# A recurrence and a two-layer product on one core: v times its factors put into the outputs' bank by transposes, the factors copied by ScalarE, the third weights' load no longer held

## The chip, the cores and the metric

One core of a Trainium2 chip runs one program. The metric is the device time of one execution in microseconds (us); the time before is the median of three runs. The profile is of a further execution, taken by the hardware profiler. Engines: PE is TensorE, DVE is VectorE, ACT is ScalarE, POOL is GpSimd, SP is SyncE, which here issues the DMAs.

## What is computed

For 4 batches and 8 heads of width 48, over 768 steps of time:

```python
for t in range(S):
    cur = einsum('bhd,bhe->bhde', u[None] * kt, vt)
    y[:, :, t] = einsum('bhd,bhde->bhe', rt, state + cur)
    state = w[None, :, :, None] * state + einsum('bhd,bhe->bhde', kt, vt)
```

The y of all heads, as 3072 tokens of 384 features, goes through `h = x @ w_in` (2048 wide), a leaky ReLU with a slope per column, and `@ w_out`.

## The kernel before, in words

**Tiling.** Time is cut into `C = 6` chunks of 128 steps, heads into `P = 4` pairs, numbered q = 0 to 3. A chunk's four pairs give the x of its 4 x 128 tokens. The 2048 columns are 16 slices of 128, each with one weights' tile of 768 KB (its piece of `w_in` and of `w_out`). Step n is one slice for one chunk's tokens: `m_in(n)` is nine 128x512 products into a bank, ACT and DVE make the activation and split it in a high and a low part (`gh`, `gl`), and `m_out(n)`, three steps later, is nine products into the accumulators `acc0` to `acc2`, in three groups of three (gh with the high weights, gh with the low ones, gl with the high ones).

**Weights.** `weights(i)` turns raw tile i, 64-bit numbers, into a high part `wh` and a low part `wl`: on ACT `wx` (L356) and `wh` (L366), on DVE L358, L360, L363 and `wl` (L367). The raw tiles have two buffers (`wraw`), so load i waits until L363 has read tile i-2. The third tile (i = 2) is held by lines 340 to 343 as well: its load stands behind the small loads of `lower` that move 16 rows of the first chunk's x.

**The first chunk**, `first_chunk(q)`, runs before any product with weights. Per pair: DVE scales r and k (L459); DVE multiplies them (L531) and eight small products with u sum that over d (`c_sum`, L538) into eight columns of the tile `bank`, the factors of v; sixteen halves of products give the scores (L469); DVE writes `vc` = v times the factors (L475) and puts the scores over the mask (`copy_predicated`, L481); `out()` then puts scores times v (L491) and `vc` times the identity (L495) in one bank y. ACT and PE split y in a high and a low part (L406, L407, L409), and the state's products follow (L298, L302, L520). `with_warm` puts a product on the identity (L236) ahead of some pieces; it writes columns 128 to 511 of the same tile `bank`, to keep the array occupied.

**The later chunks** go pair by pair through `burst`, between steps: c_sum (only chunk 1), the factors to SBUF by ACT (`cu`, L543), eight copies by ACT of the identity times a factor (`base`, L590), the last pair's state times r (L644), its scores times v (L654), this pair's state (L616) and scores (L623). Half of L654, `through_scores(1)`, waits for an ACT piece that only touches y (`seen_y`, L669). Then come the new states T (L682, L687).

**The order** of each engine is a planner's (`Plan.in_order`): every piece has a cost in us and a rank, and among pieces that could start, the lowest rank goes first. The planner also adds L236 products where it sees PE idle. On the chip each engine runs its row in this order, and waits by semaphores.

Of the kernel before, what the change touches and what calls it, by code (L numbers as in the profile page):

```python
# [8 lines left out]
F32 = mybir.dt.float32  # L9
F32R = mybir.dt.float32r  # L10
I32 = mybir.dt.int32
U8 = mybir.dt.uint8
U32 = mybir.dt.uint32
AF = mybir.ActivationFunctionType
ALU = mybir.AluOpType
AX = mybir.AxisListType

B, H, S, D = 4, 8, 768, 48
L = 128
# [11 lines left out]

MM = 0.682
WARM = 0.16

# [145 lines left out]
def rwkv_prelu_kernel(ctx: ExitStack, tc, rk, vkr, wu, u, wall, alpha, w, r_all, k_all, v_all, oT):  # L180
    nc = tc.nc
# [10 lines left out]
    plan = Plan()  # L192
    add = plan.add

    def sb(shape, name, bufs, dt=F32, pool=None):
        return plan.buf(lambda: (pool or wk).tile(shape, dt, name=name, bufs=bufs), name, bufs)
# [52 lines left out]
    def load(out, fn, kb, rank, behind=()):  # L249
# [8 lines left out]
        rank=-100)  # L258
# [62 lines left out]

    raws, first_lower = {}, []

# [11 lines left out]
    def weights(i, need):  # L335


        if i not in raws:
            p = raw_weights(i, need - 9)
            if i == 2:  # L340

                for t, at in first_lower:
                    p.after.update(o for o, part, wr in plan.log[t] if wr and part == at and o.eng == "SP")
        raw = raws[i]
        h, l, t = wh[i], wl[i], sb([128, 2 * DM], "wx", 2, U32)

        def bits():
            return t()

        def x():  # L350
            return t().bitcast(F32)

        def hx():
            return h().rearrange("p k f -> p (k f)")

        add("ACT", 0.92, lambda: nc.scalar.activation(x(), raw()[:, :, 1].bitcast(F32), AF.Abs, scale=2.0 ** -112),  # L356
            r=[raw], w=[t], rank=need - 3 - 42 * (i == 0))
        add("DVE", 0.56, lambda: nc.vector.tensor_scalar(bits(), bits(), 3, None, op0=ALU.logical_shift_left), w=[t],  # L358
            rank=need - 2 - 42 * (i == 0))
        add("DVE", 0.95, lambda: nc.vector.scalar_tensor_tensor(  # L360
            out=bits(), in0=raw()[:, :, 0], scalar=29, in1=bits(), op0=ALU.logical_shift_right, op1=ALU.bitwise_or),
            r=[raw], w=[t], rank=need - 2 - 42 * (i == 0))
        add("DVE", 0.95, lambda: nc.vector.scalar_tensor_tensor(  # L363
            out=bits(), in0=raw()[:, :, 1], scalar=0x80000000, in1=bits(), op0=ALU.bitwise_and, op1=ALU.bitwise_or),
            r=[raw], w=[t], rank=need - 2 - 42 * (i == 0))
        add("ACT", 0.85, lambda: nc.scalar.activation(hx(), x(), AF.Copy), r=[t], w=[h], rank=need - 3 - 42 * (i == 0))  # L366
        add("DVE", 0.95, lambda: nc.vector.tensor_tensor(  # L367
            out=l().rearrange("p k f -> p (k f)"), in0=x(), in1=hx(), op=ALU.subtract), r=[t, h], w=[l], rank=need - 2 - 42 * (i == 0))
# [8 lines left out]
    def lower(c, k):  # L377
        for name, t in (("xh", xh[c]), ("xl", xl[c])):
            for g in range(2):
                to = slice(HI * g + D, HI * (g + 1))  # L380

                def dma(t=t, y=top[name], g=g, to=to):
                    nc.sync.dma_start(t()[to, k].bitcast(F32), y()[HI * g + 16 * k:HI * g + 16 * (k + 1)].bitcast(F32))

                first_lower.append((t, (k, g)))
                add("SP", 0.45, dma, r=[top[name]], w=[(t, (k, g))], rank=-40 if c == 0 else -8, kb=32)
# [58 lines left out]
    def first_chunk(q):  # L445
# [12 lines left out]
        for j, (t, tab) in enumerate(((r, lambda: W[q]()[:, None, 0:L]), (k0, lambda: W[q]()[:, None, L - 1::-1]))):  # L458
            add("DVE", 0.72, lambda t=t, tab=tab: nc.vector.tensor_tensor(  # L459
                out=t(), in0=t(), in1=tab().broadcast_to([112, B, L]), op=ALU.mult),  # L460
                r=[W[q]], w=[t], rank=10 * q + j - 90)
        first = diagonal(q, r, k0, None, bank, slice(8 * q, 8 * q + 8), (bank, q), 10 * q - 88, -95 + q, -70 + q)

        A = [psum() if q % 2 == 0 else pb([128, NT], f"acc{g}") for g in range(2)]

        def scores():
# [10 lines left out]
            in0=v().rearrange("p (g b) e -> p g b e", g=2), op=ALU.mult,  # L477
            in1=bank()[:, 8 * q:8 * q + 8].rearrange("p (b g) -> p g b", g=2)[:, :, :, None].broadcast_to([128, 2, B, D])),
            r=[v, (bank, q)], w=[vc], rank=10 * q - 77)
        for g in range(2):  # L480
# [6 lines left out]
        def out():  # L487
            for b in range(B):
                for g in range(2):
                    rows, x = (slice(0, HI) if g == 0 else half(g)), g * B + b  # L490
                    nc.tensor.matmul(y()[rows, b * L:(b + 1) * L], v().rearrange("p x e -> p (x e)")[  # L491
                        :, x * D:x * D + rows.stop - rows.start], base[g]()[:, b], start=b == 0,
                        stop=False, skip_group_check=True)
            for b in range(B):
                nc.tensor.matmul(y()[0:112, b * L:(b + 1) * L], vc().bitcast(F32)[:, b, 0:112], ident(), start=False,  # L495
                                 stop=b == B - 1, skip_group_check=True)

# [31 lines left out]
    def diagonal(q, r, k0, cu, sums, cols, mine, prod_rank, sum_rank, copy_rank):  # L529
# [11 lines left out]
        first = with_warm(1 if mine != sums else 0, 0.56, c_sum, r=[prod, uw], w=[mine], rank=sum_rank)  # L541
        if cu:
            add("ACT", 0.2, lambda: nc.scalar.activation(  # L543
                cu(), sums()[:, cols].rearrange("p (b g) -> p g b", g=2), AF.Copy), r=[mine], w=[cu], rank=copy_rank)
        return first
# [450 lines left out]
```

## Time and profile before

| what | value |
|---|---|
| median of 3 runs | 490.17 us (488.49 to 490.84) |
| the profiled execution | 492.12 us, span 490.4 us |
| PE busy | 478.5 us, 98% |
| DVE busy | 312.0 us, 64% |
| ACT busy | 239.2 us, 49% |
| mean granted clock of TensorE | 0.991 |
| HBM read and written | 36.38 MB and 6.29 MB |

The span runs from the first to the last instruction of the profiled execution; 1.7 us lie around it. Times in the rows are from the span's start. A granted clock of 1.00 is 2.4 GHz, 0.50 is 1.2 GHz. Products of fp32 are recorded twice each (x8 for four), transposes once.

### The profile page before, as it was taken

The numbers are of one execution on the slowest core, as the hardware profiler recorded it, in microseconds if no ns is written. First come the engines' busy times: TensorE is split into PE (matmuls) and PEld (weight loads), VectorE is DVE, ScalarE is ACT, GpSimd is POOL, SyncE is SP. The second block draws the span as 40 slices with busy tenths as digits, with TensorE's granted clock in tenths as the row PEclk, the third lists the DMA queues.
The fourth block names the chain that finished last, engine by engine and source line by source line (L and its number), as shares of the span: only waits on it lengthen the run. The fifth ranks groups of instructions, "written<-read, shape, count | busy, mean of one in ns | idle before, by whom it ended". The sixth has DMA issues, their size and how long they took to land.

```text
span 490.4 us, 11223 instructions
## 1 busy us (share of the span) xinstructions
PE 478.5 (98%) x4650; PEld 391.7 (80%) x4650; DVE 312.0 (64%) x522; ACT 239.2 (49%) x546; POOL 45.2 (9%) x51
## 2 busy tenths in 40 slices
PE   8998999999999999999999999999999999999994
PEld 4877887888888888888888888888888878888883
DVE  6897899999966787756646646646635534333331
ACT  5287677667464454534534634534633333433332
POOL 3000020003202011101102202102000000000000
PEclk9998899999999999999999999999999999999999
DMA  7656576463153353431212321312210000100002
GB/s 240 207 140 219 191 223 205 147 218 98 48 179 89 95 168 104 142 85 34 88 52 72 117 77 44 87 43 64 72 48 1 1 1 0 65 0 0 1 0 70
DMA packets 24616, 45.82 MB, mean 93 GB/s; under 512 B 3952, under 2 KB 11504, under 8 KB 24560
## 3 DMA queue, kind: packets, MB, share of 16 engines
q1 hardware_dynamic: 24416, 44.92, 29.9%
q8 instruction: 38, 0.62, 0.5%
q14 instruction: 18, 0.15, 0.1%
q10 hardware_dynamic: 144, 0.13, 0.1%
HBM read 36.38 MB, written 6.29 MB: 87 GB/s over the span
## 4 chain that ended last, share of the span: by engine, by line
PE 89%; DMA 4%; DVE 3%; ACT 2%; SPq 1%; issue 0%; ACTq 0%; DVEq 0%
PE acc L744 40%; PE bank L710 38%; DMA wraw<-wall 3%; PE bank L644 2%; PE bank L654 2%; PE bank L623 2%; PE bank L616 1%; DMA v<-vkr 1%; PE bank L495 1%; PE bank L491 1%; SPq L421 1%; DVE wx L363 1%; ACT wx L356 1%; PE acc L469 0%; DVE wl L367 0%
## 5 line engine op out<-in xcount | busy, mean ns | idle before, releaser
L719 DVE SCALAR_TENSOR_TENSOR g<-bank,alph,g 128x512 f32<-128x512 f32 x96 | 72.0, 750 | 108.5 <-ACT g L718 107.8
L718 ACT ACTIVATE g<-bank 128x512 f32<-128x512 f32 x96 | 57.3, 596 | 140.3 <-PE bank L710 140.1
L710 PE MATMUL bank<-xh,wh 128*128 128x512 f32 x288 | 113.1, 393 | 0.0
L710 PE MATMUL bank<-xh,wl 128*128 128x512 f32 x288 | 112.3, 390 | 0.5 <-DVE wl L367 0.5
L710 PE MATMUL bank<-xl,wh 128*128 128x512 f32 x288 | 112.1, 389 | 0.0
L723 DVE TENSOR_TENSOR gl<-g,gh 128x512 fp32r<-128x512 f32 x96 | 69.6, 725 | 42.0 <-ACT gh L722 41.1
L722 ACT ACTIVATE gh<-g 128x512 fp32r<-128x512 f32 x96 | 60.6, 631 | 65.7 <-DVE g L719 65.4
L744 PE MATMUL acc<-gh,wh 128*128 128x512 f32 x288 | 84.2, 399 | 0.0
L744 PE MATMUL acc<-gh,wl 128*128 128x512 f32 x288 | 83.4, 396 | 0.0
L744 PE MATMUL acc<-gl,wh 128*128 128x512 f32 x288 | 82.4, 392 | 0.0
L744 PEld LDWEIGHTS acc<-gh,wl 128*128 128x128 f32 x288 | 54.6, 191 | 11.7
L710 PEld LDWEIGHTS bank<-xh,wl 128*128 128x128 f32 x288 | 54.2, 188 | 11.9 <-DVE wl L367 0.8
L744 PEld LDWEIGHTS acc<-gl,wh 128*128 128x128 f32 x288 | 54.3, 189 | 11.5
L710 PEld LDWEIGHTS bank<-xh,wh 128*128 128x128 f32 x288 | 54.2, 188 | 11.5 <-ACT wh L366 0.2
L710 PEld LDWEIGHTS bank<-xl,wh 128*128 128x128 f32 x288 | 54.1, 188 | 11.5
L744 PEld LDWEIGHTS acc<-gh,wh 128*128 128x128 f32 x288 | 53.2, 189 | 11.4
L579 POOL TENSOR_TENSOR rr<-rr,kk 128x384 f32<-128x384 f32 x16 | 22.6, 1410 | 290.0 <-DMA kk<-vkr 213.4
L590 ACT ACTIVATE base<-ident,cu 128x64 f32<-128x64 f32 x160 | 41.4, 337 | 3.4 <-DVE cu L585 3.3
L396 DVE TENSOR_TENSOR xl<-bank,xh 48x256 fp32r<-48x256 f32 (+1 forms) x66 | 28.4, 430 | 1.6 <-ACT xh L395 0.2
L565 DVE TENSOR_TENSOR raw<-raw,W 112x512 f32<-112x512 f32 x40 | 26.6, 682 | 1.3 <-DMA raw<-rk 1.3
L395 ACT ACTIVATE xh<-bank 48x256 fp32r<-48x256 f32 (+1 forms) x66 | 25.4, 385 | 2.2 <-PE bank L654 1.0
L654 PE MATMUL bank<-base,v 64*48 64x64 f32 x640 | 19.1, 216 | 1.8 <-ACT seen_y L669 1.8
(106 smaller groups left out, 381.4 us busy)
## 6 DMA issues: line engine op xcount, KB each, us to landing
raw<-rk SPq DMA_DIRECT2D x46, 224.0 KB, 3.5
wraw<-wall SPq DMA_DIRECT2D x10, 768.0 KB, 6.3
v<-vkr SPq DMA_DIRECT2D x24, 192.0 KB, 3.5
wraw<-wall SPq DMA_DIRECT2D x12, 384.0 KB, 3.6
rr<-vkr SPq DMA_DIRECT2D x16, 192.0 KB, 2.5
kk<-vkr SPq DMA_DIRECT2D x16, 192.0 KB, 3.4
oT<-o SPq DMA_DIRECT2D x12, 256.0 KB, 2.3
oT<-g SPq DMA_DIRECT2D x5, 256.0 KB, 2.4
```

The costliest lines, as they stand in the source:

```text
L395: add("ACT", us, lambda: nc.scalar.activation(to(h), view(), AF.Copy), r=[src], w=refs(h), rank=rank)
L396: add("DVE", us + 0.1, lambda: nc.vector.tensor_tensor(out=to(l), in0=view(), in1=to(h), op=ALU.subtract), r=[src] + refs(h), w=refs(l), r ...
L565: add("DVE", 0.72, lambda t=t, tab=tab: nc.vector.tensor_tensor(out=t().rearrange("p b (j t) -> p (b j) t", t=span), in0=t().rearrange("p ...
L579: add("POOL", 1.2, lambda: nc.gpsimd.tensor_tensor(out=rt(), in0=rt(), in1=k(), op=ALU.mult), r=[k] + ([wh[12]] if c == 2 else []), w=[rt] ...
L590: add("ACT", 0.32, lambda g=g, b=b: nc.scalar.activation(base()[:, g, b], ident2(), AF.Copy, scale=cu()[:, g, b:b + 1]), r=[cu, ident2], w ...
L654: nc.tensor.matmul(where(g, b, j), v0()[s, g * B + b], base0()[s, g, b], start=False, stop=(crossed == 1 and e == 0), skip_group_check=True)
L710: nc.tensor.matmul(hp()[:, :], a[i]()[:, k], x[c]()[:, k], start=(k == 0 and j == 0), stop=(k == NK - 1 and j == 2))
L718: add("ACT", 0.6, lambda: nc.scalar.activation(g(), hp()[:, :], AF.Copy), r=[hp], w=[g], rank=n - 100)
L719: add("DVE", 0.75, lambda: nc.vector.scalar_tensor_tensor(out=g(), in0=hp()[:, :], scalar=alph()[:, i:i + 1], in1=g(), op0=ALU.mult, op1=A ...
L722: add("ACT", 0.64, lambda: nc.scalar.activation(gh(), g(), AF.Copy), r=[g], w=[gh], rank=n - 100)
L723: add("DVE", 0.73, lambda: nc.vector.tensor_tensor(out=gl(), in0=g(), in1=gh(), op=ALU.subtract), r=[g, gh], w=[gl], rank=n - 99)
L744: nc.tensor.matmul(banks[k](), a[i]()[:, NK + k], x(), start=(begin and j == 0), stop=(end and j == 2))
```

## The change

Three things. `out()` writes `vc` into y first, by four transposes, and then adds scores times v; before, four fp32 products with the identity came last. The factors of the first chunk are copied by ACT into a tile `cu`, and DVE makes `vc` from that copy, not from `bank`. The third weights' load no longer stands behind the loads of `lower`; for tiles 2 and 3 the planner is told that they land 4 us later than its DMA model says (`late`), which changes its order alone. The diff, cut to its core (a branch for a list `BY_ACT`, which is empty, is left out, and in `weights` the reads of `raw` carry part numbers, for the planner alone):

```diff
         if i not in raws:
             p = raw_weights(i, need - 9)
-            if i == 2:
-
-                for t, at in first_lower:
-                    p.after.update(o for o, part, wr in plan.log[t] if wr and part == at and o.eng == "SP")
+            if i in (2, 3):
+                p.late = 4.0
...
-                first_lower.append((t, (k, g)))
...
-        first = diagonal(q, r, k0, None, bank, slice(8 * q, 8 * q + 8), (bank, q), 10 * q - 88, -95 + q, -70 + q)
+        cu = sb([128, 2, B], "cu", 2)
+        first = diagonal(q, r, k0, cu, bank, slice(8 * q, 8 * q + 8), (bank, q), 10 * q - 88, -95 + q, -70 + q)
...
-            in1=bank()[:, 8 * q:8 * q + 8].rearrange("p (b g) -> p g b", g=2)[:, :, :, None].broadcast_to([128, 2, B, D])),
-            r=[v, (bank, q)], w=[vc], rank=10 * q - 77)
+            in1=cu()[:, :, :, None].broadcast_to([128, 2, B, D])), r=[v, cu], w=[vc], rank=10 * q - 77)
...
         def out():
             for b in range(B):
+                nc.tensor.matmul(y()[0:112, b * L:(b + 1) * L], vc().bitcast(F32)[:, b, 0:112], ident(), start=b == 0,
+                                 stop=False, is_transpose=True, skip_group_check=True)
+            for b in range(B):
                 for g in range(2):
                     rows, x = (slice(0, HI) if g == 0 else half(g)), g * B + b
                     nc.tensor.matmul(y()[rows, b * L:(b + 1) * L], v().rearrange("p x e -> p (x e)")[
-                        :, x * D:x * D + rows.stop - rows.start], base[g]()[:, b], start=b == 0,
-                        stop=False, skip_group_check=True)
-            for b in range(B):
-                nc.tensor.matmul(y()[0:112, b * L:(b + 1) * L], vc().bitcast(F32)[:, b, 0:112], ident(), start=False,
-                                 stop=b == B - 1, skip_group_check=True)
+                        :, x * D:x * D + rows.stop - rows.start], base[g]()[:, b], start=False,
+                        stop=b == B - 1, skip_group_check=True)
...
-        if cu:
-            add("ACT", 0.2, lambda: nc.scalar.activation(
-                cu(), sums()[:, cols].rearrange("p (b g) -> p g b", g=2), AF.Copy), r=[mine], w=[cu], rank=copy_rank)
+        add("ACT", 0.2, lambda: nc.scalar.activation(
+            cu(), sums()[:, cols].rearrange("p (b g) -> p g b", g=2), AF.Copy), r=[mine], w=[cu], rank=copy_rank)
```

The change moves instructions on every engine but POOL. Line numbers after the change are 1 to 10 higher. Three places matter.

PE at pair 1 of the first chunk, with what each instruction waits for: c_sum, the product on the identity, and the scores. Before:

```order
L236 MATMUL acc_140<-ident 128x384
L538 MATMUL acc_140<-uw,g 64x2 [waits DVE_49]
L538 MATMUL acc_140<-uw,g 64x2 x7
L236 LDWEIGHTS ident
L236 MATMUL acc_140<-ident 128x384 [waits DVE_49]
L469 MATMUL acc_267<-raw 128x128 [waits DMAHW4_49,DMAHW3_49]
```

After (L237 is L236, L548 is L538, L480 is L469):

```order
L237 MATMUL acc_140<-ident 128x384
L548 MATMUL acc_140<-uw,g 64x2 [waits DVE_49]
L548 MATMUL acc_140<-uw,g 64x2 x7
L237 LDWEIGHTS ident
L237 MATMUL acc_140<-ident 128x384
L480 MATMUL acc_269<-raw 128x128 [waits DMAHW4_49,DMAHW3_49]
```

The second product on the identity waited for DVE before, and waits for nothing now (`acc_140` is the tile `bank`).

SP from the last small loads of the first chunk's x on; `v` and `raw` are the later chunks' inputs. Before:

```order
L383 DMA xl<-xl 16x512 x2
L423 DMA v<-vkr 128x384 x4
L577 DMA rr<-vkr 128x384
L327 DMA wraw<-wall 128x1536 x2
L421 DMA raw<-rk 112x512 x2
L327 DMA wraw<-wall 128x1536
```

After:

```order
L394 DMA xl<-xl 16x512 x2
L328 DMA wraw<-wall 128x1536
L433 DMA v<-vkr 128x384 x4
L586 DMA rr<-vkr 128x384
L328 DMA wraw<-wall 128x1536 x2
L431 DMA raw<-rk 112x512 x2
```

The third weights' load moved ahead of five loads; the fifth's moved ahead of two.

ACT around the second burst, from the activation copy of step 1 (`g`) on. Before:

```order
L718 ACTIVATE g<-bank 128x512
L356 ACTIVATE wx<-wraw 128x768
L302 ACTIVATE kk<-bank 128x192 x2
L722 ACTIVATE gh<-g 128x512
L669 ACTIVATE seen_y<-bank 1x2
L356 ACTIVATE wx<-wraw 128x768
```

After:

```order
L727 ACTIVATE g<-bank 128x512
L362 ACTIVATE wx<-wraw 128x768
L303 ACTIVATE kk<-bank 128x192 x2
L731 ACTIVATE gh<-g 128x512
L552 ACTIVATE cu<-bank 128x8
L696 ACTIVATE T<-T,one 112x192
L599 ACTIVATE base<-ident,cu 128x64 x5
L678 ACTIVATE seen_y<-bank 1x2
```

`seen_y` and now T stand behind the third tile's `wx` and what follows it. On PE the second step's products come partly ahead of the first burst, with two more products on the identity before them, and two groups of `m_out(0)`, not one, ahead of the second burst.

## Rows read from the trace of the kernel before

**Rows 1.** Waits of PE from 9 to 100 us: total, times, longest.

```profile
PE bank L654 <- ACT seen_y L669: 1.8, 1, 1.8
PE acc L236 <- DVE gh L475: 0.7, 1, 0.7
PE bank L710 <- DVE wl L367: 0.5, 1, 0.5
```

**Rows 2.** Stretches: busy us (instructions) of PE, PEld, DVE, ACT, POOL; clock; DMA share, GB/s.

```profile
10.00:28.00 18.00, 17.29 (x228) 14.28 (x227) 14.45 (x25) 6.63 (x15) 0.00 (x0) 1.00 0.70 216
28.00:42.00 14.00, 12.79 (x292) 10.84 (x291) 11.63 (x22) 9.55 (x28) 0.00 (x0) 1.00 0.67 206
...
44.00:51.00 7.00, 6.98 (x45) 5.69 (x46) 7.00 (x13) 5.89 (x15) 0.00 (x0) 0.55 0.52 167
51.00:60.00 9.00, 9.00 (x157) 7.53 (x156) 7.04 (x11) 4.71 (x8) 0.00 (x0) 0.97 0.48 153
60.00:100.00 40.00, 39.50 (x368) 31.63 (x367) 38.80 (x60) 28.78 (x61) 3.02 (x2) 1.00 0.67 206
100.00:400.00 300.00, 300.00 (x3094) 248.24 (x3093) 193.96 (x333) 146.85 (x352) 38.02 (x30) 1.00 0.27 80
```

**Rows 3.** The chain that ended last, 34 to 45 us: start, length, what.

```profile
34.54 7.37 DMA wraw<-wall
...
41.93 0.89 ACT wx L356
...
43.80 0.17 ACT seen_y L669
```

**Rows 4.** PE in order of time, 10 to 35 us: start, length, instructions [idle before].

```profile
10.85 0.63 PE L538 MATMUL acc<-uw,g 112*64 112x2 f32 x16
12.19 0.32 PE L236 MATMUL acc<-ident 128*128 128x384 bf16 x1 [0.71 <-DVE gh L475]
...
13.54 0.60 PE L298 MATMUL bank<-ident,raw 112*128 112x112 f32 x4
14.07 1.09 PE L491 MATMUL bank<-base,v 128*64 128x128 f32 x16
...
19.25 1.13 PE L495 MATMUL bank<-ident,gh 128*112 128x128 f32 x8
20.21 0.33 PE L236 MATMUL acc<-ident 128*128 128x384 bf16 x1
...
27.69 0.55 PE L298 MATMUL bank<-ident,o 112*128 112x112 f32 x4
28.00 0.46 PE L407 MATMUL bank<-xh,minus 112*112 112x512 f32 x1
...
34.74 0.63 PE L616 MATMUL bank<-v,kk 64*64 64x48 f32 x31 [0.82 <-ACT kk L302]
```

**Rows 5.** Groups by line and shape, 9 to 100 us: busy, mean ns | idle before.

```profile
L475 DVE TENSOR_TENSOR gh<-v,acc 128x384 f32<-128x384 f32 x4 | 2.2, 551 | 3.4 <-PE acc L236 2.1 <-PE acc L538 1.3
...
L687 ACT ACTIVATE T<-T,one 112x192 f32<-112x192 f32 x4 | 1.8, 446 | 0.0
...
L543 ACT ACTIVATE cu<-bank 128x8 f32<-128x8 f32 x4 | 0.7, 174 | 0.8 <-PE bank L538 0.8
```

**Rows 6.** The chain that ended last, 0 to 12 us.

```profile
5.03 6.46 DMA v<-vkr
```

**Rows 7.** The chain that ended last, around 102 us.

```profile
102.17 1.36 PE bank L710 x6
```

**Rows 8.** SP's queue in order of time, 29 to 36 us.

```profile
29.65 1.23 SPq L383 DMA_DIRECT2D xl<-xl  x2
30.98 3.00 SPq L423 DMA_DIRECT2D v<-vkr  x4
...
34.54 0.86 SPq L327 DMA_DIRECT2D wraw<-wall  x2
```

**Rows 9.** Line 327, the loads of whole weights' tiles.

```profile
DMA to landing us min/median/max: 4.3/7.4/9.9
```

More of the change, by code (lines that the diff above doesn't have):

```diff
@@ L32 @@
 MM = 0.682
+BY_ACT = ()
 WARM = 0.16
@@ L320, in half_table @@
             pt()[:, :].rearrange("p (m g e) -> p m g e", m=P, g=2)[:, :, :, 0:D], AF.Copy), r=[pt], w=[whalf], rank=-62)
-    raws, first_lower = {}, []
+    raws = {}
     def raw_weights(i, rank, behind=()):
@@ L354, in hx @@
             return h().rearrange("p k f -> p (k f)")
-        add("ACT", 0.92, lambda: nc.scalar.activation(x(), raw()[:, :, 1].bitcast(F32), AF.Abs, scale=2.0 ** -112),
[L357 to L362, printed above, removed]
+        early = 42 * (i == 0)
+        by_act = i in BY_ACT
+        if by_act:
+            add("ACT", 0.9, lambda: nc.scalar.activation(
+                raw()[:, :, 0].bitcast(I32), raw().rearrange("p f a -> p (f a)").bitcast(U8).rearrange("p (f a) -> p f a", a=8)[:, :, 3],
+                AF.Copy, scale=1.0 / 32, bias=-31.0 / 64), w=[(raw, 0)], rank=need - 3 - early)
+        add("ACT", 0.92, lambda: nc.scalar.activation(x(), raw()[:, :, 1].bitcast(F32), AF.Abs, scale=2.0 ** -112),
+            r=[(raw, 1)], w=[t], rank=need - 3 - early)
+        if by_act:
+            add("DVE", 0.95, lambda: nc.vector.scalar_tensor_tensor(
+                out=bits(), in0=bits(), scalar=3, in1=raw()[:, :, 0], op0=ALU.logical_shift_left, op1=ALU.bitwise_or),
+                r=[(raw, 0)], w=[t], rank=need - 2 - early)
+        else:
+            add("DVE", 0.56, lambda: nc.vector.tensor_scalar(bits(), bits(), 3, None, op0=ALU.logical_shift_left), w=[t],
+                rank=need - 2 - early)
+            add("DVE", 0.95, lambda: nc.vector.scalar_tensor_tensor(
+                out=bits(), in0=raw()[:, :, 0], scalar=29, in1=bits(), op0=ALU.logical_shift_right, op1=ALU.bitwise_or),
+                r=[(raw, 0)], w=[t], rank=need - 2 - early)
         add("DVE", 0.95, lambda: nc.vector.scalar_tensor_tensor(
             out=bits(), in0=raw()[:, :, 1], scalar=0x80000000, in1=bits(), op0=ALU.bitwise_and, op1=ALU.bitwise_or),
-            r=[raw], w=[t], rank=need - 2 - 42 * (i == 0))
+            r=[(raw, 1)], w=[t], rank=need - 2 - early)
         add("ACT", 0.85, lambda: nc.scalar.activation(hx(), x(), AF.Copy), r=[t], w=[h], rank=need - 3 - 42 * (i == 0))
```

## The prediction, on record before the changed kernel ran

> **What bounds the kernel now.** I read the waits of PE first, then a table of stretches, then the chain of waits, then the timelines of PE and SP where the change puts its hand.
>
> From 100 to 400 us PE is busy in every microsecond and the clock stands at 1.00 [rows 2]. There time is PE's own work, the change touches none of it, and whatever PE is early or late at 100 us reaches the end unchanged. So the question is what happens before 100 us.
>
> There PE has few waits: 1.8 us in a burst, until ACT has run `seen_y`; 0.7 us of a product on the identity, until DVE has made `vc`; 0.5 us for a `wl` [rows 1]; and 0.82 us ahead of the first burst [rows 4]. The first is the dear one. From 44 to 51 us, just behind it, the mean granted clock is 0.55, between the level of 2.4 GHz and that of 1.2 GHz; before and after it is 1.00 or close to it [rows 2]. Seven microseconds at 0.55 lose 7 x 0.45 = 3.2 us. The chain of waits says where it comes from: the third weights' load is issued at 34.54 and lands 7.37 us later, only then ACT can run `wx` (41.93), and `seen_y`, for which PE waits, stands in ACT's row behind that (43.80) [rows 3]. Stall and slow stretch cost 5.0 us together.
>
> DVE is the second bound. From 60 to 100 us it is busy for 38.80 of 40 us [rows 2], making weights that PE needs in turn. PE can get ahead there only as far as DVE does.
>
> **The transposes.** Four times, eight recorded products of `vc` with the identity go, and four transposes come. The eight took 0.96 us from their start to the next instruction's (19.25 to 20.21). Four transposes of 112 columns took between 0.31 us (27.69 to 28.00) and 0.53 us (13.54 to 14.07) [rows 4]; for 128 columns that is 0.35 to 0.61. Saved: 0.35 to 0.61 each, 1.4 to 2.4 in all. I take the middle of the two, 0.5 each, **2.0 us**. PE ran through this stretch without waiting, so it is PE's time. They stand first in `out()` now and wait for `vc`; but DVE writes `vc` ahead of the masked copies that L491 waited for already, so that wait is no new one.
>
> **The false wait.** L236 writes columns of `bank` that nobody else reads, yet it waited 0.71 us for DVE's `vc`, which reads other columns of that tile [rows 4], and `vc` waited for the first v, issued at 5.03 and landed 6.46 us later [rows 6]. Now ACT reads the tile, right behind c_sum; the printed order shows that product without a wait. **0.7 us.** The four copies cost ACT 174 ns each by the same copy elsewhere [rows 5]; ACT was busy for 6.63 of 18 us here [rows 2]. Without that cover each would delay the next `vc` by 0.2 us.
>
> **What DVE gets.** It sat idle 3.4 us ahead of its four `vc`. Of that 2.1 us was behind PE and goes; 1.3 us is the first v's landing, though the row names PE, and stays [rows 5].
>
> **The first burst.** PE comes 2.7 us earlier. The 0.82 us for `kk` [rows 4] were short work ahead of a busy ACT; two products on the identity, 0.33 us each [rows 4], and part of the next step stand there now. **0.2 us** gained, between 0 and 0.8.
>
> **The third weights' load.** SP issued the four v at 30.98, behind the last small load, and the weights at 34.54 [rows 8]. In the new order the weights come where the v stood, and SP's row up to there follows PE and ACT, which are some 2.5 us early: so at about 28.6. With the median landing of such loads, 7.4 us, it is there at 36.0, with the best, 4.3 us, at 32.9 [rows 9]. Before it was 41.91, so it is at least 5.9 us earlier, while PE would be earlier by 2.7 and the stall's 1.8, which is 4.5. So the load is no longer the last to come. **The 1.8 us stall goes**, and with it what the clock lost, **3.2 us**.
>
> What is late next: the printed order puts `T` behind `gh` and the factors in ACT's row, and PE's second burst begins with products that read T. From the end of c_sum that is a copy of factors, 0.17 us, and T, 0.45 us [rows 5], with the latencies some 0.75 us in which PE has nothing else (an estimate). I charge **0.75 us**, between 0 and the 1.8 of the old stall. The old waits of 0.7 and 0.82 us did not bring the clock down, so I keep it at 1.00.
>
> **DVE's cap.** Ahead of 60 us DVE is idle for 3.6 us from 10 to 28, 2.4 from 28 to 42 and 2.0 from 51 to 60 [rows 2]; less the 1.3 for the first v that is 6.7 us, and it can lose hardly more. PE already waits 0.5 us for a `wl` [rows 1]. If PE wants to be 7 us early and DVE manages 6.7, that wait grows: **0.3 us**.
>
> **Sum**: 2.0 + 0.7 + 0.2 + 1.8 - 0.75 + 3.2 - 0.3 = 6.85, say 6.9 us. The profiled execution took 492.12 us, so its like would take 485.2. It is 2.0 us above the median of 490.17; I take the same gain from the median: **483.3 us**. With all terms at their good ends (2.4, 0.7, 0.8, 1.8, 3.2, no charge) the gain is 8.9, so 481.3; with the poor ones (1.4, 0.7, 0, a new wait as long as the old stall, 3.2, and 1.0 for DVE) it is 4.3, so 485.9.
>
> The flag's path is moved too (its count on PE, three small DVE instructions, SP's load of it), to some 230 us, where PE has no wait. I cost it at nothing; SP's loads there are for bursts several steps ahead.
>
> **A rule that speaks against it.** In the trace transposes of k stand at 13.54 and at 27.69 [rows 4], in a stretch whose clock is 1.00 [rows 2]: these few did not bring it down, and I count no loss. The Trainium skill, "TensorE: Matmul & The Clock Gate", Part 4 (PE-mode transpose), says that a transpose does not count as busy for the clock as a product does. By that, 16 transposes in place of 32 recorded products thin the stretch from 12 to 28 us, and the sum would lose the 3.2 us of one slow stretch; by the rows it loses nothing.
>
> **Rivals.**
>
> *The clock falls all the same*, after the new wait for T, or among the transposes. For it: it fell once after 1.8 us without work. Against: shorter gaps left it alone. The price is the 3.2 us of rows 2, the gain 6.9 - 3.2 = 3.7: 486.5 us. Where the transposes alone are the cause (the page's rule above), the price and the time are the same. 18 in 100, of which 5 are for the rule.
>
> *The transposes cost what the products did.* An fp32 product is recorded twice; if these transposes are as well, 2.0 falls away: gain 4.9, 485.3 us. Against: all transposes in the trace are recorded once [rows 4]. 6 in 100.
>
> *The first v comes late: no gain, or slower.* The third weights' 768 KB now lie ahead of the v that the first burst needs. PE was at that burst at 34.74 - 0.82 = 33.9; it comes 2.7 earlier, but with two products on the identity (0.66), a c_sum (0.63 [rows 4]) and six products of the next step (1.36 [rows 7]) put ahead, so at 33.9 again. If the weights take 7.4 us (36.0 [rows 9]) and this v's 128x384 numbers 0.9 us more at 216 GB/s [rows 2], PE stands for 3.0 us, and the clock falls there instead. Then 2.7 early, 0.82 for the old wait and 1.8 for the old stall stand against 0.66, 3.0 and 0.75, and the 3.2 stays lost: a gain of 0.9, 489.3 us. Each microsecond more costs one: from a v that lands after 37.8 on, the kernel is slower than before; with the longest landing, 9.9 us, v is there at 39.4 and the time is 491.8 us. For it: the median landing. Against: that median stems from loads issued next to others, while this one has SP's queue nearly to itself; 4.3 us and a v at 33.8 are nearer. 9 in 100, of which 4 end slower by over 0.5%.
>
> **How the numbers follow.** The main case has 67 in 100 and lies from 481.3 to 485.9. The range for 8 in 10 takes it whole, with the dear transposes and the clock's case, whose own ends are as far apart: 480.5 to 488.5; the 0.8 below is for the profiled execution's distance from the median, half of which may be time that the median never lost or lost elsewhere. 0.5%, 2.45 us, is about what a measurement of this kernel can tell from no change. Faster by more (below 487.7) are the main case, the dear transposes and 11 of the clock's 18: 0.84. The same are 7 of the clock's and 5 of the late v's: 0.12. Slower: 0.04.
>
> **What would show it.** Right: the four transposes at the head of each `out()` recorded once; L236 without a wait for DVE near 12 us; the third weights landed before ACT's `wx` wants them; no PE wait near 42 us over 1 us, a short one on T; clock 1.00 from 10 to 100 us; PE in 100 to 400 full, all 7 us earlier. Wrong: a clock under 1.00 in any of these stretches; PE waiting for v or `kk` at the first burst; waits for `wl` above 1 us from 50 to 80 us, which would say that DVE caps it lower.

## The result and the profile after

| | before | changed |
|---|---|---|
| median | 491.17 us (488.49 to 492.61, 6 runs) | **484.77 us** (484.29 to 485.34, 6 runs) |
| the profiled execution | 492.12 us, span 490.4 | 485.22 us, span 483.4 |
| mean granted clock | 0.991 | 0.996 |

The ratio is 0.9873, interval [0.9843, 0.9903]: faster by 1.0 to 1.6%. The forecast of 483.3 us was 1.5 us too low, and the measured median lies inside its range. The profiled execution gained 6.90 us, where the sum had 6.85; the runs below show that several of its terms had other sizes or did not come, so that the sum came out this near is in part luck.

The waits of PE from 9 to 100 us in the changed kernel (total, times, longest), where [rows 1] stood:

```profile
PE bank L299 <- ACT T L535: 0.4, 1, 0.4
PE bank L663 <- ACT seen_y L678: 0.2, 1, 0.2
PE bank L504 <- DVE base L491: 0.2, 1, 0.2
PE bank L499 <- DVE gh L486: 0.2, 1, 0.2
```

The 1.8 us for `seen_y` and the 0.7 for `vc` at the product on the identity are gone. The stretches of [rows 2], same columns:

```profile
10.00:28.00 18.00, 17.68 (x264) 13.97 (x264) 16.57 (x27) 9.39 (x23) 0.00 (x0) 1.00 0.81 228
28.00:42.00 14.00, 13.56 (x266) 10.85 (x265) 13.20 (x26) 11.97 (x37) 0.00 (x0) 1.00 0.56 193
...
44.00:51.00 7.00, 7.00 (x146) 5.85 (x145) 6.93 (x11) 3.78 (x8) 0.00 (x0) 1.00 0.91 283
51.00:60.00 9.00, 9.00 (x84) 7.13 (x84) 8.35 (x14) 7.71 (x19) 0.79 (x1) 1.00 0.83 230
60.00:100.00 40.00, 39.68 (x334) 32.46 (x329) 38.79 (x56) 26.47 (x51) 1.96 (x2) 1.00 0.61 194
100.00:400.00 300.00, 300.00 (x3149) 247.35 (x3148) 193.02 (x333) 145.64 (x354) 36.58 (x30) 1.00 0.25 77
```

The clock stands at 1.00 in every one; what is left under 1.00 is the tail (0.50 from 480 us on), after PE's last product, while the last results are stored. DVE is now busy for 16.57 of the 18 us from 10 to 28 (14.45 before): more of its work falls into this stretch.

PE in order of time, pair 1 of the first chunk and both bursts (start, length, instructions, [idle before]), where [rows 4] stood:

```profile
14.84 0.34 PE L237 MATMUL acc<-ident 128*128 128x384 bf16 x1
...
17.03 0.65 PE L499 MATMUL bank<-ident,gh 128*112 128x128 f32 x4
17.60 1.09 PE L504 MATMUL bank<-gl,v 128*64 128x128 f32 x16
...
34.30 0.62 PE L625 MATMUL bank<-v,kk 64*64 64x48 f32 x30
...
38.07 0.63 PE L548 MATMUL bank<-uw,g 112*64 112x2 f32 x16
38.63 1.14 PE L653 MATMUL bank<-raw,T 48*48 48x64 f32 x32
```

The four transposes take 0.57 us from their start to the next instruction's. The first burst (34.30) starts without a wait, and so does the second: the products that read T (38.63) follow c_sum directly. DVE's T of the first burst, then ACT around the second burst, same columns:

```profile
35.90 0.40 DVE L691 SCALAR_TENSOR_TENSOR T<-T,one,bank 112x192 f32<-112x192 f32 x1
```

```profile
36.88 0.89 ACT L362 ACTIVATE wx<-wraw 128x768 f32<-128x768 f32 x1
...
38.83 0.45 ACT L696 ACTIVATE T<-T,one 112x192 f32<-112x192 f32 x1
...
40.49 0.17 ACT L678 ACTIVATE seen_y<-bank 1x2 f32<-1x2 f32 x1
```

The third weights (issued at 28.98, SP's row) are there before ACT wants them at 36.88: no wait ahead of `wx`, where ACT before had to wait for them until 41.93 [rows 3].

### The profile page after: what moved, and what is told of

The parts are those of the page before. It is cut to its first block, busy times and chain, and to the rows that moved or that the text cites. A ratio compares the mean times of both kernels' runs of the same rounds, so it can differ in the third digit from the quotient of the medians.

```text
span 483.4 us, 11208 instructions
## 1 busy us (share of the span) xinstructions
PE 474.7 (98%) x4636; PEld 387.6 (80%) x4636; DVE 313.0 (65%) x522; ACT 238.5 (49%) x550; POOL 42.9 (9%) x51
## 4 chain that ended last, share of the span: by engine, by line
PE 93%; DMA 2%; DVE 2%; ACT 1%; SPq 1%; issue 0%; ACTq 0%; DVEq 0%
PE acc L753 41%; PE bank L719 40%; PE bank L653 3%; PE bank L663 2%; PE bank L632 2%; PE bank L625 2%; DMA v<-vkr 1%; SPq L431 1%; PE bank L504 1%; PE bank L548 0%; DMA xl<-xl 0%; PE bank L299 0%; ACT xl L419 0%; ACT wh L377 0%; ACT kk L303 0%
## 5 line engine op out<-in xcount | busy, mean ns | idle before, releaser
L753 PE MATMUL acc<-gh,wl 128*128 128x512 f32 x288 | 82.0, 391 | 0.0
L588 POOL TENSOR_TENSOR rr<-rr,kk 128x384 f32<-128x384 f32 x16 | 20.2, 1265 | 285.3 <-DMA kk<-vkr 196.3
L574 DVE TENSOR_TENSOR raw<-raw,W 112x512 f32<-112x512 f32 x40 | 27.7, 711 | 2.8 <-DMA raw<-rk 2.8
L684 DVE COPY_PREDICATED base<-strict,bank 128x256 f32<-128x256 uint8 x40 | 17.2, 441 | 4.7 <-PE bank L632 4.4
```

The source lines that it names most:

```text
L588: add("POOL", 1.2, lambda: nc.gpsimd.tensor_tensor(out=rt(), in0=rt(), in1=k(), op=ALU.mult), r=[k] + ([wh[12]] if c == 2 else []), w=[rt] ...
L684: add("DVE", 0.42, lambda g=g: nc.vector.copy_predicated(base()[:, g], strict2()[:, None, :].broadcast_to([128, B, HI]), A[g]()[:, 0:256]. ...
L753: nc.tensor.matmul(banks[k](), a[i]()[:, NK + k], x(), start=(begin and j == 0), stop=(end and j == 2))
```

## The experiments

The kernel before is run again beside each group, and its own median moves: 490.22 (32 runs), 490.55 (23 runs), 489.51 (11 runs). It is read against the mean granted clock of each execution. Where that is 0.996 or more, before took 488.0 to 488.6 us; at 0.993 or 0.994 mostly 488.6 to 490.1; at 0.989 to 0.991 mostly 490.2 to 492.9. The changed kernel has 0.995 or 0.996 in all six, and they lie within 1.1 us. Whether an execution without a profile had a slow stretch, a stretch of several us at 0.50 before PE's last product, is inferred from this mean: of the fourteen profiles of this document, the nine with a mean of 0.996 or more have none, and the five with 0.990 to 0.995 have one each. So there are two things to explain: some 3.3 us between executions with no slow stretch, and what slow stretches add to the median. Since before's median moves, kernels are compared below by their own times. By the ratios a difference can come out a microsecond larger: the transposes are 2.2 us by them and not 0.95, with intervals that overlap.

**The transposes.** The changed kernel with products in their place; every engine's order stays.

```diff
-                                 stop=False, is_transpose=True, skip_group_check=True)
+                                 stop=False, skip_group_check=True)
```

> The changed kernel with the four products of vc with the identity in the transposes' place, first in out(); the order of every engine is the changed kernel's, row for row. Theory (a transpose is cheaper than two passes of an fp32 product): out() is 0.4 to 0.5 us longer for each of the four pairs, so PE comes 1.6 to 2.0 us later to the first step and the time is 486.4 to 486.8 against 484.8. Rival 1 (DVE caps PE between 50 and 80 us, PE's time in the prelude is slack): the four are longer in the trace but the time moves by less than 0.7. Rival 2 (transposes cost what products cost): no difference in the trace either. The clock stays at 1.00 from 10 to 100 us by all of them.

Measured: 485.72 us (485.09 to 487.52, 9 runs), ratio to before 0.9917 [0.9891, 0.9943]. PE at pair 1, in order of time:

```profile
16.96 1.13 PE L499 MATMUL bank<-ident,gh 128*112 128x128 f32 x8
18.01 1.09 PE L504 MATMUL bank<-gl,v 128*64 128x128 f32 x16
```

1.05 us against 0.57: nearly half a microsecond at a pair, as the prediction had it, 1.9 in four. But the median is lower than expected, 0.95 us above the changed kernel's, and the first `m_in` starts at 30.21 and not 28.84 (1.4 us). Pair 0 gives nothing: PE waits there 0.15 and 0.17 us for DVE's `gh` and `base` in the changed kernel, behind the first v's landing, and not at all in this one, whose pair 0 is done at 14.77 (the changed kernel's at 14.84, shown above):

```profile
14.77 0.34 PE L237 MATMUL acc<-ident 128*128 128x384 bf16 x1
```

Pairs 1 to 3 give 0.48 each, which is the 1.4. The ninth step's `m_in` starts at 80.96 and not 79.96 (1.0), so half of the 1.9 is lost by 80 us; where the 0.4 between pair 3 and the ninth step goes was not followed. The clock is 1.00 from 10 to 400 us in both kernels: sixteen transposes in place of thirty-two recorded products cost no slow stretch. So what the prediction worked out from the rule that it weighed (the Trainium skill, "TensorE: Matmul & The Clock Gate", Part 4: a transpose does not count as busy for the clock as a product does) does not come out here.

**The hold put back.** The changed kernel with the third weights held as before, and without `late`; the orders are then those of the kernel before, but for `out()` and ACT's copies.

```diff
-            if i in (2, 3):
-                p.late = 4.0
+            if i == 2:
+                for t, at in first_lower:
+                    p.after.update(o for o, part, wr in plan.log[t] if wr and part == at and o.eng == "SP")
```

> The changed kernel's transposes and ScalarE copies, with the third weights' load held as before and the planner not told of a later landing; the orders are the kernel before's but for out() and the copies. Theory (two separate gains, a short prelude and an early load): the load is issued some 2.5 us earlier only because the prelude is shorter, PE still stands near 40 us for seen_y for 1.5 to 2 us, the clock falls behind that, and the gain is the prelude's 2.5 to 3.0: 488.2 to 488.7 against 491.2. Rival 1 (the shorter prelude is what takes the stall away): no stall, clock at 1.00, 485 to 486. Rival 2 (transposes thin the work by which the clock is kept up): the clock falls already before 35 us and the time is 490 or more.

Measured: 486.32 us (484.28 to 489.82, 12 runs), 0.9931 [0.9902, 0.9959]. Six executions at a clock of 0.996 to 0.998 took 484.3 to 485.8, as the changed kernel does; the other six, at 0.991 to 0.995, 486.8 to 489.8. The waits of PE in the profile, an execution of 485.44 us:

```profile
PE bank L419 <- ACT xh L418: 0.7, 1, 0.7
PE bank L665 <- ACT seen_y L680: 0.6, 1, 0.6
```

**This did not come out as the prediction had it.** The stall of 1.8 us is mostly gone although the load is still held. ACT and SP show why. The first row is of ACT, the second of SP:

```profile
37.33 0.92 ACT L363 ACTIVATE wx<-wraw 128x768 f32<-128x768 f32 x1 [0.80 <-DMA wraw<-wall]
```

```profile
31.03 0.86 SPq L328 DMA_DIRECT2D wraw<-wall  x2
```

The load stands in the same place of SP's row, yet is issued 3.5 us earlier than in before [rows 8]: 2.5 us since the first chunk is earlier (the four v start at 28.52 and not 30.98), and 1.0 since the four v ahead of it take SP 1.95 us and not 3.00. It also lands in 6.3 us, not 7.4. PE is ready for the second burst's L654 3.4 us earlier (38.8 against 42.2), the load is there 4.6 us earlier (37.33 against 41.93), and so 0.6 us of the 1.8 are left. The earlier first chunk alone would not do it, since it brings the load 2.5 us forward and PE comes 3.4 us earlier; what makes up the difference is the quicker issue and the quicker landing. In before, SP paused for 1.3 us among the four v; its waits put that down to PE's L710, which is inferred. In the three profiles of the kernel with the hold put back the four take 1.95 us, without a pause; in the four with before's `out()` and the held load 3.00, 3.87, 1.95 and 2.89. Whether the earlier first chunk is what takes the pause away stays open.

To find an execution with a slow stretch, two more were profiled.

> The changed kernel with the third weights' load held again, as before, for a second profile: half of its executions took 484.3 to 485.8 us and half 486.8 to 489.8 at a lower mean clock, and the first profile was of a fast one. If the stall of the held load is what brings the clock down, a profiled execution of over 486.5 us shows a clock under 1.00 between 38 and 51 us, right behind a wait for seen_y or for an xh of 1.5 us or more, and 1.00 from 10 to 38 us. Rival: the clock falls in the first chunk, between 10 and 28 us, as it did without the factors' copies. An execution under 486 us shows no stretch under 1.00 before the end of TensorE's work.

> A third profile of the same kernel, with the same expectations: over 486.5 us a clock under 1.00 between 38 and 51 us behind a wait of 1.5 us or more; under 486 us none.

They took 484.61 and 485.86 us, with a clock of 1.00 from 10 to 100 us and `seen_y` waits of 0.8 and 0.4 us. In none of three profiles did the clock fall, so where it falls in this kernel's other executions stays open.

**The early load alone.** The kernel before, with the hold taken out and `late` put in as in the diff; nothing else.

```diff
-            if i == 2:
-                for t, at in first_lower:
-                    p.after.update(o for o, part, wr in plan.log[t] if wr and part == at and o.eng == "SP")
+            if i in (2, 3):
+                p.late = 4.0
```

> The kernel before with only the hold on the third weights' load taken away and the planner told of a later landing of tiles 2 and 3; its prelude is untouched, the later orders are the changed kernel's. Theory: the load lands before ACT wants it, the 1.8 us stall and the slow stretch behind it (3.2 us at the profile's figure) go, a new wait of up to 0.75 us comes: 486.5 to 487.5 against 491.2, clock 1.00 from 10 to 100 us. Rival (the load was one of several late things, and with a prelude 2.7 us longer something else, the v of the first burst behind 768 KB of weights, stalls PE): a wait of over 1 us at the first burst near 35 us, perhaps a slow stretch there, and 489 to 491.

Measured: 489.01 us (487.72 to 490.36, 12 runs), 0.9979 [0.9955, 1.0003]. Hardly a gain. Waits of PE, and two stretches:

```profile
PE acc L236 <- DVE gh L473: 1.3, 1, 1.3
PE bank L614 <- DMA v<-vkr: 1.0, 1, 1.0
PE bank L652 <- ACT seen_y L667: 0.6, 2, 0.4
```

```profile
10.00:28.00 18.00, 16.67 (x204) 13.65 (x202) 13.00 (x22) 5.08 (x12) 0.00 (x0) 0.91 0.65 193
44.00:51.00 7.00, 7.00 (x161) 5.95 (x158) 6.59 (x11) 5.70 (x16) 0.00 (x0) 1.00 0.57 178
```

The stall at the second burst is down to 0.6 us in two pieces, and the clock is 1.00 behind it. Instead the false wait of the first chunk is 1.3 us in this execution, and the clock falls behind that; and the first burst waits 1.0 us for a v that now stands behind the weights. That is a third of what the third rival had, and it is not shown to be its mechanism: two runs below, where the v stand ahead of the weights, wait 1.6 and 1.2 us for it. This run brought the theory of two places: either wait can bring the clock down, and which one does changes from execution to execution.

**The false wait put back** (called false because the two touch different columns of the tile; whether it could be left out no run shows). The changed kernel, with `vc` made from the bank again and no copies by ACT.

```diff
-        cu = sb([128, 2, B], "cu", 2)
-        first = diagonal(q, r, k0, cu, bank, ...
+        first = diagonal(q, r, k0, None, bank, ...
...
-            in1=cu()[:, :, :, None].broadcast_to([128, 2, B, D])), r=[v, cu], w=[vc], rank=10 * q - 77)
+            in1=bank()[:, 8 * q:8 * q + 8]...), r=[v, (bank, q)], w=[vc], rank=10 * q - 77)
```

> The changed kernel with vc made straight from the bank tile and no copies by ScalarE; PE's and SP's orders are the changed kernel's. Theory (the false wait of the product on the identity behind vc costs PE 0.7 us at pair 1): L236's waits for DVE come back, 0.5 to 0.8 us at 12 us, and the time is 485.3 to 485.6 against 484.8. Rival 1 (the first v's landing holds pair 0's transposes in any case, so the wait only moves): the wait is in the trace, the transposes' own wait of 0.15 us goes, and the time moves by less than 0.3. Rival 2 (vc stands later for each pair, as it now waits for PE's product too): more than 1 us.

Measured: 487.56 us (485.09 to 490.42, 12 runs), 0.9952 [0.9927, 0.9978]: 2.8 us more than the changed kernel, from a wait that the prediction put at 0.7. PE's wait, and the first microseconds by stretches (same columns as above):

```profile
PE acc L237 <- DMA v<-vkr: 1.1, 1, 1.1
```

```profile
12.00:13.00 1.00, 0.35 (x3) 0.10 (x2) 0.96 (x2) 0.00 (x0) 0.00 (x0) 1.00 1.06 412
13.00:14.00 1.00, 1.00 (x17) 0.88 (x17) 1.00 (x3) 0.00 (x0) 0.00 (x0) 1.00 1.04 420
14.00:16.00 2.00, 2.00 (x14) 1.66 (x13) 2.00 (x4) 0.55 (x2) 0.00 (x0) 0.52 1.09 274
16.00:18.00 2.00, 2.00 (x21) 1.53 (x20) 1.29 (x3) 0.28 (x1) 0.00 (x0) 0.62 0.98 318
```

PE stands until 12.65 and is full from there on; the clock goes to half speed at about 14 and comes back before 18. From 14 to 18 us that is 2 x 0.48 + 2 x 0.38 = 1.7 us lost, besides the 1.1 of the wait. Together that is 2.8, which is also the difference of the medians; that the two agree is in part chance, as this kernel's executions lie anywhere from 485.1 to 490.4.

**The copies alone.** The kernel before with ACT's copies, the same lines the other way round.

> The kernel before with only ScalarE's copies of the factors in the first chunk; products with the identity, the held load and the planner's landing stay, PE's, SP's rows are those of before. Theory (the false wait is where the first v's late landing reaches PE, 0.7 to 1.3 us, and in some executions the clock falls behind it): the wait at 12 us is gone, the clock is 1.00 from 10 to 28 us in every execution, the gain is the wait's 0.7 plus part of the clock's share, 1 to 2.5 us: 487.7 to 489.2 against 490.2. Rival 1 (the stall in the second burst alone brings the clock down): 0.7, 489.5, and the lowest executions are no lower than before's 488.0. Rival 2 (the copies lie on the path): no gain.

Measured: 488.32 us (486.54 to 492.89, 12 runs), 0.9951 [0.9921, 0.9981]. The profile is of an execution of 492.58 us:

```profile
PE bank L654 <- ACT seen_y L669: 2.5, 1, 2.5
PE bank L616 <- DMA v<-vkr: 1.6, 1, 1.6
```

```profile
10.00:28.00 18.00, 18.00 (x240) 14.78 (x238) 15.03 (x25) 7.82 (x19) 0.00 (x0) 1.00 0.73 219
44.00:51.00 7.00, 6.17 (x42) 5.11 (x43) 6.96 (x13) 6.30 (x17) 0.00 (x0) 0.56 0.43 155
```

The first chunk runs without a gap, and the stall of the second burst is there in full, with its slow stretch. The 1.6 us ahead of the first burst, near 34 us, bring no fall by themselves: the clock stands at 1.00 from 36 to 42 us.

**The stall filled.** The kernel before with eight products of zeros, which add nothing to the accumulators, put where PE stood for `seen_y`.

```diff
+            if was == 0:
+                x = ident().bitcast(mybir.dt.bfloat16)
+                for _ in range(8):
+                    nc.tensor.matmul(A[0]()[:, :].rearrange(...), x[:, 0:1].broadcast_to([128, 128]), ...
```

> The kernel before with eight bf16 products by a zero matrix, 512 columns each, put into PE's row between the second burst's products and the part of it that waits for seen_y; they add nothing to a bank. No wait is taken away; they fill some 1.75 us of a stall of 1.8. Theory (the clock falls because PE stands idle there): the slow stretch from 44 to 51 us goes, in the profile and in most executions; 488.0 to 489.0 against 490.2 while the wait for seen_y's row is as late as before. Rival (the clock falls for another reason, the thin products of the burst or the stretch before, or the prelude's wait does it): the clock falls as often as before, 490 to 491.

Measured: 490.8 us (488.3 to 492.53, 12 runs), 0.9995 [0.9968, 1.0023]: nothing. The profile:

```profile
PE acc L236 <- DVE gh L475: 2.2, 1, 2.2
```

```profile
10.00:28.00 18.00, 15.81 (x177) 12.92 (x178) 11.36 (x20) 3.33 (x6) 0.00 (x0) 0.81 0.63 190
44.00:51.00 7.00, 7.00 (x126) 5.20 (x121) 5.66 (x9) 6.05 (x16) 0.00 (x0) 1.00 0.48 135
```

Behind the filled stall the clock is 1.00, but the false wait is 2.2 us in this execution and 18 x 0.19 = 3.4 us are lost behind it.

**Both places closed**: the last two edits together, without transposes and without the early load. It is the run that decides.

> The kernel before, with ScalarE's copies of the factors in the first chunk and with the eight zero products in the second burst's stall; no transposes, no early load. Theory of two places: the false wait of the prelude and the stall of the second burst each bring the clock down in a part of the executions, and closing one alone leaves the other (the copies alone gave 488.3 us, the filling alone 490.8, before 490.6). Both closed: clock 1.00 in all stretches from 10 to 100 us of the profile, 0.995 or more over the whole in at least 9 of 12 executions, a median of 487.3 to 488.3 us, what before takes in its best executions (488.0 to 488.3) less the 0.5 of the false wait. Rival, that the clock falls somewhere in the first 60 us whatever these two places do: a third place shows a clock under 1.00, most executions stay at 0.991 to 0.994, and the median is 489.5 to 490.5.

Measured: 487.45 us (486.84 to 489.25), 0.9944 [0.9923, 0.9965], in six executions. All six have a clock of 0.996 to 0.998; of before's eleven beside it none has over 0.994. Both stretches of the profile:

```profile
10.00:28.00 18.00, 17.95 (x229) 14.49 (x225) 14.75 (x25) 7.61 (x18) 0.00 (x0) 1.00 0.76 217
44.00:51.00 7.00, 6.75 (x58) 5.36 (x59) 6.99 (x12) 5.00 (x15) 0.00 (x0) 1.00 0.75 225
```

Either edit alone left most executions with a mean clock under 0.996 (seven of twelve with the copies, eleven of twelve with the filling), both together none of six. The rival, a fall whatever these two places do, does not fit that. The median holds the zeros themselves: 1.90 us in PE's row, however long the stall is.

**Small parts of the change, and what is left.** First the changed kernel with `late` at 0.

> The changed kernel with the planner not told that tiles 2 and 3 land later. It puts ACT's wx of tile 2 ahead of gh, the factors and base of the first burst, ACT reaches it near 32.6 us, and the load is issued at 29.0. Theory (a wrong landing in the plan makes ACT's row wait and PE behind it): ACT waits 0.5 to 3 us for the load near 33 us, PE waits over 1 us before 42 us, and the time is 486 to 489 with the clock down in some executions. Rival 1 (the load lands by 33 us): no wait, and as DVE gets its weights earlier 484 to 485. Rival 2 (the new order of m_out and the bursts matters more): waits elsewhere, for T or seen_y.

Measured: 485.12 us (484.63 to 486.69, 6 runs), 0.9888 [0.9849, 0.9926], next to the changed kernel's 0.9873: no difference that can be measured. ACT waits 0.87 us for the load, until 33.32, but no wait of PE from 9 to 100 us is over 0.4, and the clock stands at 1.00: the order that was feared costs nothing that shows. Then the changed kernel without the products on the identity that fill the first chunk (`range(n)` made `range(0)` in `with_warm`).

> The changed kernel without the eight products on the identity that stand ahead of pieces of the first chunk (0.27 us each, 2.1 us of PE); all orders are otherwise the changed kernel's. It computes the same. Theory (half of PE's own time in the prelude comes through, as with the transposes, 1.0 of 1.6 us): 483.6 to 484.2 against 484.8, clock 1.00. Rival 1 (these products keep the clock up across the waits of the prelude): the clock falls between 8 and 30 us in some executions and the time is 485.5 to 488 with a wide spread. Rival 2 (the first v's landing and DVE bound the prelude): within 0.3 of 484.8.

Measured: 484.98 us (484.29 to 485.72, 6 runs), 0.9881 [0.9844, 0.9919]. PE's first `m_in` comes 0.65 us earlier and its eighteenth step 0.8, but at the end only 0.3 is left. PE has one wait from 100 to 480 us, where the changed kernel's profile names none:

```profile
PE bank L653 <- DVE g L728: 0.6, 1, 0.6
```

This was taken for too much work on DVE. DVE's row says otherwise: just before that `g` it stood for a later chunk's `raw`, a load, 3.10 us here and 1.67 us in the changed kernel:

```profile
138.37 1.42 DVE L574 TENSOR_TENSOR raw<-raw,W 112x512 f32<-112x512 f32 x2 [3.10 <-DMA raw<-rk]
```

```profile
138.03 0.69 DVE L574 TENSOR_TENSOR raw<-raw,W 112x512 f32<-112x512 f32 x1 [1.67 <-DMA raw<-rk]
```

A version with less for DVE was tried: that kernel, with ACT taking one of DVE's shifts in the third to fifth weights (`BY_ACT = (2, 3, 4)`).

> The changed kernel without the products that keep the array occupied in the first chunk, and with ScalarE taking one of VectorE's two shifts in the conversion of the third to fifth weights' tiles, which the code can do by its list BY_ACT. Theory that VectorE is what takes back PE's lead between 50 and 200 us (without the products PE was 0.8 us earlier at 120 us and lost 0.6 of it in a wait for VectorE's activation near 190 us): three times 0.4 to 0.95 us less on VectorE lets the lead stand, 484.0 to 484.5 us. Rival, that ScalarE, which also stands ahead of VectorE in the conversion, becomes the late one: a wait for ACT's wx or wh from 45 to 70 us and 485.0 to 486.0.

Measured: 484.46 us (483.89 to 484.93, 6 runs), 0.9884 [0.9864, 0.9905]. No wait of PE from 100 us on is left, but one of 0.9 for DVE's `g` at 59.5 has come. DVE's waits for that `raw` are 0.20 and 0.49 us in this execution, so the run does not show that less work on DVE is what took the wait away. By its ratio it is the changed kernel's equal: nothing here beats it by what a measurement can tell.

## Why the prediction was right or wrong

**The transposes, 2.0 us**: right per piece (0.48 saved by 0.57 against 1.05), wrong at the end: 0.95 us in the medians, though the medians do not settle it to a microsecond. The step that failed is that PE ran through this stretch without waiting, *so it is PE's time*. At pair 0 it is not: there DVE, behind the first v, is no longer ahead, and the transposes give nothing. Another 0.4 us of the three other pairs' 1.4 is gone by the ninth step. The charge of 0.3 for DVE was put at a later stretch, as a longer wait for `wl`; the changed kernel's profile has no such wait from 9 to 100 us. The rival that they cost what the products did is out.

**The false wait, 0.7 us**: the mechanism held, the wait is gone, and the size failed. It is no fixed 0.7: in the profiles that have it, it was 0.7, 1.1, 1.3 and 2.2 us, since it ends with a DMA; and behind the three longer ones the clock fell. Put back, it cost 2.8. The sentence that failed is *the old waits of 0.7 and 0.82 us did not bring the clock down*: true of the one execution that was profiled, and read as true of the kernel.

**The stall 1.8 and the clock 3.2, by the early load**: both went, but the load's place is not what took most of them away. With the load held, but the first chunk changed, the stall fell to 0.4 to 0.8 us in three profiles, as the load came earlier by more than PE did (4.6 us against 3.4 in the first), and executions without a slow stretch were as quick as the changed kernel; what the early load adds is that none of 33 executions of the five kernels with it and the copies had a mean clock under 0.995, where six of the twelve timed with the load held took 486.8 to 489.8 us at 0.991 to 0.995: 486.32 to 484.77, 1.55 us. Alone it was worth 1.2 us (490.22 to 489.01), at the edge of what can be told. The step that failed is the line of argument from [rows 3] to the hold: the profile showed that the load ended last, not that its place in SP's row was the reason. The clock's 3.2 us were 3.4 in that profile: seven us at 0.55 and nine at 0.97.

**The new wait for T, -0.75 us**: it did not come, and the reading behind it was wrong. The second burst's products start at 38.63, where c_sum ends, and ACT's `T`, which was to hold them, starts at 38.83. They do not read that one: in the kernel it is the state for the pair's next chunk. The T that they read come from before the first burst and from DVE's L691, at 35.90.

**The first burst, 0.2 us**: its wait is gone, as forecast. The third rival's late v does not show in the changed kernel. It shows in the early load alone (1.0 us), but also where the v stand ahead of the weights (1.6 us in the copies alone, 1.2 with both places closed), so the weights are not its only reason.

**From 100 us on.** *Whatever PE is early or late at 100 us reaches the end unchanged* holds but for half a microsecond. By the starts of the steps PE is 2.4 us early at the first `m_in`, 7.8 at 100 us and 7.0 at its end. Of the 0.8 between, 0.4 is the flag's product, which stands at 224.9 us and not at 86.8 any more, so it is moved and not lost. The other 0.4 goes between 127 and 149 us, most of it just behind DVE's wait of 1.67 us for `raw`; the kernel with products, where that wait is 0.33, does not lose it. PE is busy in every microsecond there by the table, so such a loss does not show in a busy share.

**From the profiled execution to the median.** The sum stood against 492.12 us and gave 485.2; the like of it took 485.22. Then *I take the same gain from the median*, and that is the step that made 483.3 too low: the profiled execution of before held a whole slow stretch, and not every execution does. The changed kernel has none to lose, so its median lies at its profiled time, and the gain on medians is smaller: 490.17 to 484.77 is 5.4 us by the times shown before, 6.4 by the six runs beside the changed kernel.

**The gain in steps.** Executions with a clock of 0.996 or more, by their medians: before 488.1 (six of 55 beside the first eight experiments), with the copies 487.2 (five of twelve), with copies and transposes 485.1 (six of twelve, the load held), the changed kernel 484.8 (all six, one of them at 0.995). So some 3.3 us are work and waits on PE's path, nearly all of it by the first chunk's two edits, and by this reckoning the other 2 to 3 us of the median are slow stretches. Such a choice by the clock also chooses executions whose loads came early, so the steps are rough: the transposes are 2.1 us in this row and 0.95 in the order of the changed kernel.

## What to carry to other kernels

Where a wait ends with a DMA, its length in one profile is one draw: look at the spread of times and clocks over the executions before you price it, and set the sum against the median only after you have asked which terms every execution pays. Where two waits can each bring the clock down, closing one shows little; try both together before you drop either. A load that ends last can be late by its place on the queue, by a pause in the issues ahead of it or by its landing, and one profile does not tell which: here three of the four profiles with the load held and before's `out()` had a pause among the v ahead of it.

## What the runs showed of the hardware that was not expected

- A wait of 1.1 us near 12 us was followed by a fall of the clock to half (put back, the false wait), while longer ones near 34 us were not: 1.6 us in the copies alone (shown there), and 1.2 us with both places closed, at the first burst:

```profile
PE bank L616 <- DMA v<-vkr: 1.2, 1, 1.2
```

  The length of a wait alone does not price it.
- The clock can fall behind the wait and not in it. With the false wait put back PE was busy again from 12.65 us, and the stretch from 13 to 14 still stood at 1.00; the slow stretch then lies over full work. It need not be so: with the stall filled, the clock was already at 0.84 from 12 to 13 us, where PE stood all the time (its wait of 2.2 us ended at 13.00).

```profile
12.00:13.00 1.00, 0.00 (x0) 0.00 (x0) 0.60 (x2) 0.00 (x0) 0.00 (x0) 0.84 1.05 418
```
